# Layer norm's mean moved from the activations into the output weights, z's lower halves on VectorE, and a new order of the first phase

## The chip, the cores and the metric

One Trainium2 chip, one of its cores. The metric is the device time of one launch in microseconds (us); three runs of the kernel before gave 1175.65, 1175.5 and 1172.25 us, median 1175.5 us. Engines: PE (TensorE, matrix products), DVE (VectorE), ACT (ScalarE), POOL (GpSimd), and SP (SyncE), which issues the DMAs.

## The reference, cut to what matters

```python
def _moe_ref(x, w_in, w_out, g_ln):          # x: 4608 x 512, the attention's output
    h = x @ w_in                             # 4608 x 1024
    e = np.exp(h - np.max(h, axis=-1, keepdims=True))
    sm = e / (np.sum(e, axis=-1, keepdims=True) + 1e-09)
    solu = h * sm
    mu = np.mean(solu, axis=-1, keepdims=True)
    var = np.mean((solu - mu) ** 2, axis=-1, keepdims=True)
    ln = (solu - mu) / np.sqrt(var + 1e-06) * g_ln
    return ln @ w_out                        # 4608 x 512

def _moe2_ref(x, w_in, w_out):
    h = x @ w_in                             # 4608 x 2048
    return (h / (1 + np.exp(-1.702 * h))) @ w_out
```

Ahead of `_moe_ref` stands attention of 8 batches x 8 heads over keys and values pooled by 8; `_moe2_ref` takes its output. Inputs come in float64 for the weights, which the kernel takes as pairs of 32-bit words.

## The kernel before, in words

**Two phases.** The first does the attention, the first layer (`_moe_ref`) and the preparation of the second layer's weights; its 4608 tokens go in 36 tiles of 128, and two tiles make a `Pair`. The second phase is the second layer, in 6 blocks of 768 tokens, as products of 2x2 blocks by a seven-product scheme; its instructions have lines of their own (L1385 for its matrix products), and its program is written out by hand.

**Products in halves.** A float32 operand is split into a float16 upper half (`hi`) and a float16 lower half (`lo`, what the upper one leaves), and a product is three float16 products (`PASSES`). A product of float32 operands, used for scores and for sums over the pooled keys, appears as two records in the trace.

**One tile of the first phase.** Scores on PE into bank `psx`; softmax on DVE, ACT and POOL; the split attention goes through a transposing DMA (`aT`); PE makes the attention's output in `psv`; ACT and DVE split it into `xT`. `Pair.hidden` multiplies `xT` by `w1i` into one of two banks `psh` (24 products), DVE takes the row maximum `hmx` and its scaled negative `nm`, ACT the exponential `he`, DVE the product `tt` and its sum `mean`, ACT the sum of squares `vs`. `Pair.norm` makes the factor `a` on POOL, column by column of two; then, for each tile, ACT writes `tt = a * tt + mean` (mean is by then multiplied by -a), ACT copies the upper half into `zs[:, 0]`, and the lower half is a subtraction on POOL or DVE, whichever the planner finds free first. A transposing DMA turns both tiles' `zs` into `zT`, and `Pair.project` multiplies it by the output weights `w1o` (four groups of 24 products in a pair) into bank `psy`, near the end of the phase every second half into `psv`. There is one `psy`; the pooled sums of keys and values of batches 1 and 2 use it too, as do some of the products with `ones` that spread a maximum over the partitions.

**The output weights.** `second_weight` loads `w_out` in four parts, joins the words of each (`joined`, ending on POOL), finds the largest value, and `first_half` writes `w1o` for eight blocks of 128 rows: upper half on ACT, scaled by `gs` (g times the power of two), lower half on DVE.

**The order.** The first phase is put in order when the program is built. Each piece of work is a `Strand` of operations; `Plan.run` repeatedly takes the operation with the lowest score, made of the start that the planner's costs give, of the strand's due time, and of a random draw. `DRAWS` lists stretches of planned time with the size and the seed of the draw. So any edit to an operation, a cost or a seed changes the order on all engines. Each engine and SP's queue then work strictly in that order. On one line each, all operations of this phase are emitted by `op` (L496), `D` (L528) and `T` (L537), so that the profile tells them apart by their tiles only.

Of the kernel before, what the change touches and what calls it, by code (L numbers as in the profile page):

```python
# [84 lines left out]
DRAWS = ((70e3, 600, 13), (200e3, 150, 4), (330e3, 150, 13), (1e9, 150, 1))  # L85
# [4 lines left out]
LN_UP = 2.0 ** 10  # L90
# [93 lines left out]
class Plan:  # L184
# [13 lines left out]
    def start(self, steps, due):  # L198
        s = Strand(self, steps, due)
        self.strands.append(s)  # L200
        return s
# [95 lines left out]
def moe_kernel(ctx: ExitStack, tc: tile.TileContext, qT, kT, vT, w_in, w_out, g_ln, w2_in, w2_out, eye, outT):  # L297
# [138 lines left out]
    with ExitStack() as ph:  # L436
# [22 lines left out]
        def until(*strands):  # L459
            return lambda: all(s.ended for s in strands)  # L460
# [257 lines left out]
        def second_weight(due):  # L718
            n = 4
            am, a1, alln, gs = s1("w1o_am", n), s1("w1o_a1"), s1("w1o_all"), s1("w1o_gs", K1)  # L720
            measured = [None] * n

            def scale():
                yield lambda: all(measured)
                yield V("tensor_reduce", out=a1, in_=am, axis=AX.X, op=ALU.max)
                yield from largest(a1, alln, WIDE_LEAST)
                yield from whole_scale(alln, w1o_up, w1o_dn)
                yield g_done.over
                yield V("tensor_scalar_mul", gs, g_col, w1o_up)

            def part(i):
                raw = yield raw_new(2, DM)
                yield raw_load(raw, w_out, i, DM, 2)
                join = start(joined(raw.rearrange("p q f t -> p (q f) t"), lambda: measured[i]), due + 4 * i)
                two = [
                    start(
                        first_half(
                            join, raw[:, j], scaled.over, gs[:, 2 * i + j : 2 * i + j + 1], 2 * i + j,
                            slice(0, WC), w1o,
                        ),  # L740
                        due + 4 * i,
                    )
                    for j in range(2)
                ]

                def measure():
                    yield absmax_op(am[:, i : i + 1], high_words(raw), axis=AX.XY)
                    measured[i] = True

                start(measure(), DUE_MAX_OUT)  # L750
                yield until(*two)
                drop(raw)

            scaled = start(scale(), due)
            yield until(*[start(part(i), due + 4 * i) for i in range(n)])

# [69 lines left out]
        def values(b, due):  # L826
# [3 lines left out]
            yield from largest(am, alln, TINY, b < 2)  # L830
# [123 lines left out]
        class Pair:  # L954
# [53 lines left out]
            def norm(self):  # L1008
# [10 lines left out]
                yield G("tensor_tensor", out=q, in0=q, in1=q, op=ALU.mult)  # L1019
                yield G("tensor_tensor", out=v, in0=q, in1=self.vs, op=ALU.add)  # L1020
                yield G("tensor_tensor", out=r, in0=v, in1=minus_half, op=ALU.pow)
# [4 lines left out]
                yield G("tensor_tensor", out=self.mean, in0=self.mean, in1=a, op=ALU.mult)  # L1026
# [3 lines left out]
                for j in range(2):  # L1030
                    s = slice(j, j + 1)
                    tt = self.tt[j]
                    yield A(out=tt, in_=tt, func=AF.Identity, scale=a[:, s], bias=self.mean[:, s])
                    zs = yield New(sb, [P, 2, DF1], F16, "zs", bufs=2)
                    yield A(out=zs[:, 0], in_=tt, func=AF.Copy)
                    yield VG("tensor_tensor", out=zs[:, 1], in0=tt, in1=zs[:, 0], op=ALU.subtract)
                    drop(tt)
                    both.append((zs, (self.zT[:, :, j * P : (j + 1) * P], zs.rearrange("p a c -> p (a c)"))))
# [686 lines left out]
```

## Time and profile before

| | |
|---|---|
| runs | 1175.65, 1175.5, 1172.25 us; median 1175.5 us |
| the profiled execution | 1171.0 us, of it 1169.0 us from the first to the last instruction (the span) |
| PE busy in the span | 1125.7 us (96%) |
| DVE, ACT, POOL busy | 724.4, 754.7, 617.7 us (62%, 65%, 53%) |
| first phase, last product of a `zT` | ends at 510.7 us |
| granted clock of PE, mean | 0.994 |

A tile is named by the program's name without its number. `x8` behind an instruction is a count. In a list over time the bracket at the end tells how long the engine had been idle before and what ended that; in a list of groups, the two numbers after the bar are the busy time in us and the mean of one in ns. Matrix products are pipelined, so that one in a run takes less than its own mean.

### The profile page before, as it was taken

What the parts mean: (1) busy time and instruction counts of PE and PEld (TensorE: products, weight loads), DVE (VectorE), ACT (ScalarE), POOL (GpSimd) and SP (SyncE); (2) the same over time, 40 slices, a digit from 0 to 9 for tenths busy, and PEclk for the clock granted to TensorE, in tenths of its full rate; (3) what the DMA queues carried; (4) which work ended last, traced back from release to release, by engine and by line L of the source; (5) the groups of instructions that cost most, each with busy time, mean ns of one, the idle gap of its engine ahead of it and who ended that gap; (6) DMA issues with size and microseconds to landing.
All of it is one profiled execution on the core that took longest, in us unless ns stands there. A gap on an engine that the chain in (4) does not pass through costs nothing.

```text
span 1169.0 us, 19696 instructions
## 1 busy us (share of the span) xinstructions
PE 1125.7 (96%) x7737; PEld 726.1 (62%) x7737; DVE 724.4 (62%) x1105; ACT 754.7 (65%) x997; POOL 617.7 (53%) x643
## 2 busy tenths in 40 slices
PE   4888999999999999999999999999999999999998
PEld 4555676667676667765566656666666665566655
DVE  7988888777677753426753773567266636753650
ACT  6889998989798874737624752674367337625740
POOL 4566999989999985315503530561056016403530
PEclk9989999999999999999999999999999999999999
DMA  9979999999999768355465355536453653463131
GB/s 356 277 191 278 243 280 282 278 275 273 270 244 226 178 172 262 85 195 193 146 200 174 125 176 163 180 127 202 142 174 126 214 178 127 149 202 117 60 121 60
DMA packets 247356, 225.75 MB, mean 193 GB/s; under 512 B 165728, under 2 KB 218080, under 8 KB 246752
## 3 DMA queue, kind: packets, MB, share of 16 engines
q1 hardware_dynamic: 247264, 224.50, 67.0%
q8 instruction: 60, 0.98, 0.3%
q14 instruction: 32, 0.26, 0.1%
HBM read 151.06 MB, written 33.55 MB: 158 GB/s over the span
## 4 chain that ended last, share of the span: by engine, by line
PE 69%; POOL 13%; ACT 6%; DVE 5%; DMA 5%; issue 2%; SPq 1%; POOLq 0%; ACTq 0%; DVEq 0%
PE bank_a L1385 31%; PE bank_d L1385 16%; PE bank_b L1385 8%; PE psy L537 6%; PE psh L537 5%; POOL w_f L496 3%; PE psv L537 2%; POOL lo L496 2%; POOL zs L496 2%; POOL st L496 1%; POOL e L496 1%; PE psx L537 1%; DMA w2i_dram<-lo 1%; POOL q L496 1%; DMA raw<-w_out 1%
## 5 line engine op out<-in xcount | busy, mean ns | idle before, releaser
L1385 PEld LDWEIGHTS <-w2o 128*128 128x128 f16 x2016 | 197.0, 98 | 130.4
L1385 PEld LDWEIGHTS <-w2i 128*128 128x128 f16 x1974 | 193.1, 98 | 129.9 <-issue 2.4
L349 POOL TENSOR_TENSOR w_g<-w_g 128x384 f32<-128x384 f32 x42 | 46.1, 1097 | 399.2 <-ACT w_g L1464 399.2
L1479 DVE SCALAR_TENSOR_TENSOR g<-w_g,gu_b,g 128x1152 f16<-128x1152 f32 (+1 forms) x96 | 175.4, 1828 | 92.0 <-ACT g L1474 91.7
L1385 PE MATMUL bank_a<-ys,w2i 128*128 128x384 f16 x1128 | 205.6, 326 | 0.9 <-ACT c L1404 0.9
L537 PE MATMUL psh<-w1i,xT 128*128 128x512 f16 x864 | 201.8, 384 | 3.5 <-ACT xT L496 3.1
L1385 PE MATMUL bank_a<-g,w2o 128*128 128x384 f16 x1152 | 201.6, 326 | 0.0
L537 PEld LDWEIGHTS <-w1o 128*128 128x128 f16 x1728 | 168.0, 98 | 30.8 <-DMA zT<-zs 2.8
L537 PE MATMUL psy<-zT,w1o 128*128 128x256 f16 x1536 | 176.2, 273 | 3.5 <-DMA zT<-zs 2.3
L1474 ACT ACTIVATE g<-w_g,gu_b 128x1152 f16<-128x1152 f32 (+1 forms) x96 | 134.3, 1411 | 50.3 <-POOL w_g L352 39.3
L1404 ACT ACTIVATE c<-bank_a 128x384 f32<-128x384 f32 x188 | 90.7, 483 | 102.4 <-PE bank_a L1385 101.8
L537 PEld LDWEIGHTS <-xT 128*128 128x128 f16 x864 | 83.4, 99 | 96.3 <-issue 6.0
L1385 PE MATMUL bank_d<-g,w2o 128*128 128x384 f16 x576 | 104.2, 326 | 0.0
L496 POOL TENSOR_TENSOR zs<-tt,zs 128x1024 f16<-128x1024 f32 x36 | 78.4, 2178 | 44.2 <-ACT zs L496 43.8
L1385 PE MATMUL bank_d<-ys,w2i 128*128 128x384 f16 x564 | 101.1, 326 | 0.0
L1464 ACT ACTIVATE w_g<-c,ch_b 128x1536 f32<-128x1536 f32 x47 | 73.8, 1570 | 28.7 <-DVE c L1407 28.7
L352 POOL TENSOR_TENSOR w_g<-w_g 128x384 f32<-128x384 f32 x42 | 83.2, 1982 | 0.0
L1407 DVE SCALAR_TENSOR_TENSOR c<-bank_d,c 128x384 f32<-128x384 f32 x94 | 51.9, 552 | 41.9 <-ACT c L1404 29.6
L496 POOL TENSOR_TENSOR lo<-w_f,hi 128x512 f16<-128x512 f32 (+1 forms) x48 | 65.8, 1389 | 6.6 <-ACT e L496 2.9
L496 DVE TENSOR_REDUCE hmx<-psh 128x1 f32<-128x1024 f32 x36 | 43.8, 1218 | 36.2 <-PE psh L537 36.2
L537 PE MATMUL psx<-kbd,qt 128*128 128x144 f32 (+1 forms) x320 | 47.8, 312 | 15.1 <-ACT kbd L496 9.6
L496 DVE CUSTOM_DVE_ANT_0 tt<-psh,he 128x1024 f32<-128x1024 f32 x36 | 43.8, 1218 | 23.1 <-ACT he L496 22.9
(205 smaller groups left out, 1606.8 us busy)
## 6 DMA issues: line engine op xcount, KB each, us to landing
w2i<-w2i_dram SPq DMA_DIRECT2D x48, 896.0 KB, 4.6
w2o<-w2o_dram SPq DMA_DIRECT2D x84, 512.0 KB, 3.7
half<-kT SPq DMA_DIRECT2D x16, 576.0 KB, 6.4
half<-vT SPq DMA_DIRECT2D x16, 576.0 KB, 6.2
qt<-qT SPq DMA_DIRECT2D x36, 256.0 KB, 4.7
y_dram<-y SPq DMA_DIRECT2D x36, 256.0 KB, 3.5
y<-y_dram SPq DMA_DIRECT2D x48, 192.0 KB, 4.0
raw<-w_in SPq DMA_DIRECT2D x16, 512.0 KB, 7.7
```

The lines of the kernel that those rows point to most:

```text
L349: eng.tensor_tensor(out=w[:, 1], in0=q[:, Q12], in1=q[:, Q11], op=ALU.subtract)
L352: eng.tensor_tensor(out=w[:, 3], in0=q[:, Q21], in1=w[:, 2], op=ALU.subtract)
L496: getattr(eng, name)(*args, **kw)
L537: nc.tensor.matmul(*p[:3], start=p[3], stop=p[4], skip_group_check=len(p) > 5)
L1385: nc.tensor.matmul(bank, self.weight(p, kk, w), self.data(p, kk, i), start=(first and kk == 0 and w == 0 and i == 0), stop=(last and kk == ...
L1404: nc.scalar.activation(out=self.c[:, i], in_=getattr(self, bank), func=AF.Copy, scale=self.scale)
L1407: nc.vector.scalar_tensor_tensor(out=self.c[:, i], in0=getattr(self, bank), scalar=self.scale, in1=self.c[:, i], op0=ALU.mult, op1=ALU.add,)
L1464: nc.scalar.activation(out=self.w[:, 0:4], in_=self.c, func=AF.Gelu_apprx_sigmoid, scale=self.ch)
L1474: nc.scalar.activation(out=self.g[s.start][:, 0], in_=self.w[:, s], func=AF.Copy, scale=self.gu)
L1479: nc.vector.scalar_tensor_tensor(out=self.g[s.start][:, 1], in0=self.w[:, s], scalar=self.gu, in1=self.g[s.start][:, 0], op0=ALU.mult, op1 ...
```

## The change

Three things are changed in the first phase; the second phase's text is the same.

1. `second_weight` no longer scales and splits each part by itself. After the parts are joined, ACT writes `g_rows` (minus g over 1024, each value broadcast over 128 columns), PE multiplies it with the joined weights in eight float32 products of 128 x 512 into `psy`, so that every row of `psy` holds minus the column mean of g times w_out. ACT scales that by `w1o_up`. For each of the eight blocks DVE then writes the weight times `gs` plus `psy`, ACT copies the upper half, and POOL or DVE subtracts for the lower half. `psy` is given back after the last block.
2. `Pair.norm` no longer subtracts the mean: the pass `tt = a * tt + mean` is gone, ACT's copy into `zs[:, 0]` has the scale `a`, and the lower half is a `scalar_tensor_tensor` on DVE alone (tt times a minus the upper half). On POOL the product of mean and a is gone; a square of the mean and two short steps that keep the variance above a floor come in ahead of the power.
3. `DRAWS` has other stretches and seeds, a spread maximum of the output weights and of the second batch's values uses `psv` instead of `psy`, and `LN_UP` is 1.

```diff
-DRAWS = ((70e3, 600, 13), (200e3, 150, 4), (330e3, 150, 13), (1e9, 150, 1))
+DRAWS = ((70e3, 600, 5), (400e3, 150, 5), (430e3, 150, 813651), (1e9, 150, 495492))
...
-LN_UP = 2.0 ** 10
+LN_UP = 1.0
+LEVEL = 2.0 ** -18
...
-                yield from largest(a1, alln, WIDE_LEAST)
+                yield from largest(a1, alln, WIDE_LEAST, False)
...
-            def part(i):
+            def load(i):
                 raw = yield raw_new(2, DM)
                 yield raw_load(raw, w_out, i, DM, 2)
-                join = start(joined(raw.rearrange("p q f t -> p (q f) t"), lambda: measured[i]), due + 4 * i)
-                two = [
-                    start(
-                        first_half(
-                            join, raw[:, j], scaled.over, gs[:, 2 * i + j : 2 * i + j + 1], 2 * i + j,
-                            slice(0, WC), w1o,
-                        ),
-                        due + 4 * i,
-                    )
-                    for j in range(2)
-                ]
+                joins.append(start(joined(raw.rearrange("p q f t -> p (q f) t"), lambda: measured[i]), due + 4 * i))
+                words[i] = raw
...
+            yield g_done.over
+            rows = yield New(kv, [P, K1, P], F32, "g_rows", bufs=1)
+            yield A(out=rows, in_=g_col.unsqueeze(2).to_broadcast([P, K1, P]), func=AF.Copy, scale=-1.0 / DF1)
+            yield lambda: len(joins) == n and joins[0].ended
+            ps = yield New(psy, [P, 2, YB], F32, "psy", "psy")
+            level = ps.rearrange("p a c -> p (a c)")
+            for i in range(n):
+                yield joins[i].over
+                yield T(
+                    [
+                        (level, rows[:, 2 * i + j], words[i][:, j, :, 0].bitcast(F32), i + j == 0, i + j == n)
+                        for j in range(2)
+                    ]
+                )
+            drop(rows)
+            yield scaled.over
+            yield A(out=level, in_=level, func=AF.Copy, scale=w1o_up)
+
+            def levelled(i, j):
+                k = 2 * i + j
+                word = words[i][:, j, :, 0].bitcast(F32)
+                yield V(
+                    "scalar_tensor_tensor", out=word, in0=word, scalar=gs[:, k : k + 1], in1=level, op0=ALU.mult,
+                    op1=ALU.add,
+                )
+                yield A(out=w1o[0][:, k], in_=word, func=AF.Copy)
+                yield VG("tensor_tensor", out=w1o[1][:, k], in0=word, in1=w1o[0][:, k], op=ALU.subtract)
...
-            yield from largest(am, alln, TINY, b < 2)
+            yield from largest(am, alln, TINY, b < 1)
...
+                yield G("tensor_tensor", out=r, in0=self.mean, in1=self.mean, op=ALU.mult)
                 yield G("tensor_tensor", out=v, in0=q, in1=self.vs, op=ALU.add)
+                for j in range(2):
+                    s = slice(j, j + 1)
+                    yield G(
+                        "tensor_scalar", out=v[:, s], in0=r[:, s], scalar1=LEVEL, scalar2=v[:, s], op0=ALU.mult, op1=ALU.max
+                    )
...
-                yield G("tensor_tensor", out=self.mean, in0=self.mean, in1=a, op=ALU.mult)
...
-                    yield A(out=tt, in_=tt, func=AF.Identity, scale=a[:, s], bias=self.mean[:, s])
                     zs = yield New(sb, [P, 2, DF1], F16, "zs", bufs=2)
-                    yield A(out=zs[:, 0], in_=tt, func=AF.Copy)
-                    yield VG("tensor_tensor", out=zs[:, 1], in0=tt, in1=zs[:, 0], op=ALU.subtract)
+                    yield A(out=zs[:, 0], in_=tt, func=AF.Copy, scale=a[:, s])
+                    yield V(
+                        "scalar_tensor_tensor", out=zs[:, 1], in0=tt, scalar=a[:, s], in1=zs[:, 0], op0=ALU.mult,
+                        op1=ALU.subtract,
+                    )
```

Where the order moves: DVE's queue of before, at the place where the output weights' lower halves are written. `raw` is a part of `w_out`, `w1o_130` the lower halves, `mx` and `e` belong to the scores of a tile, `ISA tt` is the product with the exponential.

```order
L496 TENSOR_SCALAR w1o_gs<-g_col,w1o_up 128x8
L496 ISA tt,mean<-psh,he 128x1024
L496 ISA mean 128x1
L496 SCALAR_TENSOR_TENSOR w1o_130<-raw,w1o_gs,w1o_129 128x512 x8
L496 TENSOR_TENSOR e<-psx,mx 128x576
L496 TENSOR_SCALAR mean<-mean 128x1
L496 TENSOR_REDUCE hmx<-psh 128x1
L496 TENSOR_SCALAR nm<-hmx,h_sc 128x1
```

DVE's queue now, at the same work: the eight blocks read `psy` and are spread among scores and lower halves `zs`.

```order
L497 SCALAR_TENSOR_TENSOR zs<-tt,a,zs 128x1024
L497 SCALAR_TENSOR_TENSOR xT<-psv,xT 128x512
L497 TENSOR_SCALAR nm<-hmx,h_sc 128x1
L497 RECIPROCAL rs<-rs 128x8
L497 ISA tt,mean<-psh,he 128x1024
L497 ISA mean 128x1
L497 TENSOR_SCALAR mean<-mean 128x1
L497 SCALAR_TENSOR_TENSOR xT<-psv,xT 128x512
L497 SCALAR_TENSOR_TENSOR raw<-raw,w1o_gs,psy 128x512 x2
L497 TENSOR_REDUCE mx<-psx 128x8
L497 TENSOR_TENSOR e<-psx,mx 128x576
L497 SCALAR_TENSOR_TENSOR raw<-raw,w1o_gs,psy 128x512 x2
```

The first of the eight now stands behind a scaling on ACT, and with it behind the eight products on PE; two of the `zs` have come ahead of it.

ACT's queue of before, at the end of the first phase: `y` copies a projection out of its bank, `ys` are the second phase's first tokens, `c_kept` results of its first products.

```order
L496 ACTIVATE ys<-w_y_5978,y_up 128x4x384
L496 ACTIVATE y<-psy 128x512
L496 ACTIVATE ys<-w_y_5979,y_up 128x4x384
L496 ACT_TABLE_LOAD
L496 ACTIVATE ready<-y_up 128x1
L496 ACTIVATE y<-psv 128x512
L496 ACTIVATE c_kept<-psx 128x384 x2
L496 ACTIVATE y<-psy 128x512
L496 ACTIVATE y<-psv 128x512
L496 ACTIVATE c_kept<-psx 128x384 x2
```

ACT's queue now, at the same place.

```order
L497 ACTIVATE ys<-w_y_6173,y_up 128x4x384
L497 ACTIVATE ys<-w_y_6174,y_up 128x4x384
L497 ACT_TABLE_LOAD
L497 ACTIVATE ready<-y_up 128x1
L497 ACTIVATE y<-psy 128x512
L497 ACTIVATE y<-psv 128x512
L497 ACTIVATE c_kept<-psx 128x384 x4
```

Two of the second phase's first results stood ahead of the last pair's projection; now all four stand behind it.

## Rows read from the trace of the kernel before

**Rows 1.** Stretches: length; busy PE, PEld, DVE, ACT, POOL; PE clock; DMA share; GB/s
```profile
0.00:102.00 102.00, 72.86 (x478) 50.58 (x478) 87.87 (x168) 82.57 (x120) 56.96 (x70) 0.95 0.96 276
102.00:500.00 398.00, 388.78 (x3150) 273.90 (x3151) 274.24 (x502) 328.08 (x474) 336.34 (x406) 1.00 0.96 238
570.00:1169.00 599.00, 595.57 (x3663) 357.89 (x3661) 328.13 (x401) 303.16 (x355) 192.03 (x143) 1.00 0.46 151
```
**Rows 2.** PE in order of time, 88 to 117 us: start, us, what
```profile
102.08 5.41 PE L537 MATMUL psy<-zT,w1o 128*128 128x256 f16 x48 [2.34 <-DMA zT<-zs]
107.43 0.64 PE L537 MATMUL psv<-aT,vst 128*64 128x128 f16 x16
107.99 1.25 PE L537 MATMUL psx<-kbd,qt 128*128 128x144 f32 x8
```
**Rows 3.** What PE waited for, 102 to 570 us: total us, times, longest
```profile
PE psv L537 <- DVE xT L496: 3.9, 5, 1.7
PE psv L537 <- DVE w2all L496: 2.2, 1, 2.2
PE psx L537 <- ACT c_kept L496: 0.6, 1, 0.6
```
**Rows 4.** PE in order of time, 54 to 61 us: float32 products of the pooled sums
```profile
55.74 4.08 PE L537 MATMUL psy<-half,eye_t 128*128 128x144 f32 x32
```
**Rows 5.** Groups by form, 0 to 560 us: count | busy us, mean ns | idle before
```profile
L496 ACT ACTIVATE tt<-tt,mean,a 128x1024 f32<-128x1024 f32 x36 | 44.5, 1237 | 1.9 <-POOL mean L496 1.8
L496 ACT ACTIVATE zs<-tt 128x1024 f16<-128x1024 f32 x36 | 38.0, 1054 | 0.6
L496 ACT ACTIVATE vp<-psy 128x288 f32<-128x288 f32 x2 | 0.8, 406 | 0.5 <-PE psy L537 0.5
L496 POOL TENSOR_TENSOR zs<-tt,zs 128x1024 f16<-128x1024 f32 x36 | 78.4, 2178 | 44.2 <-ACT zs L496 43.8
L496 POOL TENSOR_TENSOR lo<-w_f,hi 128x512 f16<-128x512 f32 x32 | 37.9, 1192 | 6.5 <-ACT e L496 2.9 <-ACT rs L496 2.4 <-DMA w2i_dram<-lo 1.2
L496 POOL TENSOR_SCALAR q<-hsm 128x2 f32<-128x2 f32 x18 | 5.4, 301 | 1.5
L496 DVE SCALAR_TENSOR_TENSOR raw<-raw 128x1024 int32<-128x1024 int32 x22 | 34.0, 1546 | 3.3 <-ACT raw L496 3.3
L496 DVE TENSOR_REDUCE w2am<-raw 128x1 f32<-128x1024 f32 x16 | 19.3, 1209 | 3.8 <-DMA raw<-w_out 3.8
L496 DVE SCALAR_TENSOR_TENSOR xT<-psv,xT 128x512 f16<-128x512 f32 x36 | 24.7, 687 | 12.4 <-ACT xT L496 12.1
L496 DVE SCALAR_TENSOR_TENSOR w1o<-raw,w1o_gs,w1o 128x512 f16<-128x512 f32 x8 | 5.4, 744 | 0.0
L496 DVE TENSOR_TENSOR e<-psx,mx 128x576 f32<-128x576 f32 x35 | 26.4, 755 | 3.5 <-POOL st L496 2.2
L496 DVE TENSOR_REDUCE vam<-vp 128x1 f32<-128x288 f32 x8 | 3.5, 434 | 0.0
L496 DVE TENSOR_SCALAR pw_v<-v_all 128x1 int32<-128x1 int32 x8 | 1.2, 151 | 0.1
```
**Rows 6.** ACT in order of time, 74 to 83 us
```profile
73.40 1.20 ACT L496 ACTIVATE he<-psh,nm,h_sc 128x1024 f32<-128x1024 f32 x1
77.12 5.38 ACT L496 ACTIVATE w1o<-raw,w1o_gs 128x512 f16<-128x512 f32 x8 [2.42 <-DVE w1o_gs L496]
```
**Rows 7.** DVE and POOL in order of time, 399 to 402 us
```profile
399.75 2.22 DVE L496 SCALAR_TENSOR_TENSOR raw<-raw 128x1024 int32<-128x1024 int32 x1
...
399.74 1.15 POOL L496 TENSOR_TENSOR e<-e,rs 128x576 f32<-128x576 f32 x1 [0.24 <-ACT raw L496]
400.84 1.18 POOL L496 TENSOR_TENSOR q<-q 128x2 f32<-128x2 f32 x1
```
**Rows 8.** Stretches, columns as in Rows 1
```profile
29.00:117.00 88.00, 74.77 (x549) 49.67 (x549) 79.11 (x166) 78.26 (x117) 53.29 (x69) 0.94 0.99 249
146.00:292.00 146.00, 142.47 (x1148) 100.33 (x1146) 114.36 (x204) 129.29 (x189) 136.66 (x161) 1.00 1.10 278
```

More of the change, by code (lines that the diff above doesn't have):

```diff
@@ L720, in second_weight @@
             am, a1, alln, gs = s1("w1o_am", n), s1("w1o_a1"), s1("w1o_all"), s1("w1o_gs", K1)
-            measured = [None] * n
+            measured, words = [None] * n, [None] * n
             def scale():
@@ L750, in part @@
                 start(measure(), DUE_MAX_OUT)
+            joins = []
+            scaled = start(scale(), due)
+            for i in range(n):
+                start(load(i), due + 4 * i)
+            yield g_done.over
[4 more added lines that the diff above has]
+            level = ps.rearrange("p a c -> p (a c)")
+            for i in range(n):
+                yield joins[i].over
[17 more added lines that the diff above has]
+                yield VG("tensor_tensor", out=w1o[1][:, k], in0=word, in1=w1o[0][:, k], op=ALU.subtract)
+            for i in range(n):
+                two = [start(levelled(i, j), due + 4 * i) for j in range(2)]
                 yield until(*two)
-                drop(raw)
-            scaled = start(scale(), due)
-            yield until(*[start(part(i), due + 4 * i) for i in range(n)])
+                drop(words[i])
+            drop(ps)
         BY_PRODUCT = (1, 2)
```

## The prediction

> **What bounds the kernel now.** I read the busy time by stretches first, then PE over time around the first projection, then what PE waited for. The stretches [rows 1] show two regimes. From 102 us on PE is hardly ever idle: 388.8 of 398 us up to 500, and 595.6 of 599 in the second phase, whose text the change leaves alone. Up to 102 us it is idle for 29.1 of 102 us, and there DVE (87.9) and ACT (82.6) are the busy ones. The hinge is the first projection, at 102.08 us [rows 2]; from there on PE has enough work in stock. So the time is PE's work, plus what PE idles until its stock is filled, plus 9.2 us of small waits later, half of which DVE ends: 3.9 us in five waits for `xT`, 2.2 us in one for a maximum of the second weights [rows 3]. The large sums that the change takes off ACT and POOL are not on this path after 102 us; they count only where they bring the first projection forward or end one of the small waits.
>
> **What is removed, off the path.** ACT loses 36 passes of 1.24 us, 44.5 us; its copy gets a scale, and so takes between the copy's 1.05 and the old pass's 1.24 us, at most 6.6 us in all. POOL loses 36 subtractions of 2.18 us, 78.4 us [rows 5]. In the norm one short POOL step goes and three come, 0.6 us a pair at 0.30 each [rows 5]; the chain from the sums to `zs` loses far more than that. I take nothing for all this directly: PE hides it, being busy. If that cover went, a `zs` chain would be shorter by about 2 us (1.24 and the 0.63 to 0.97 between POOL's 2.18 and the price on DVE, below, less 0.6).
>
> **The lower halves on DVE.** No row has this operation with both operands of these types. The nearest is the join of raw words, also 128 x 1024 with two operands in SBUF: 1.55 us on the mean [rows 5]. Below, a pass over 1024 columns is 1.21 us (`w2am`); above, one join took 2.22 us beside a busy POOL [rows 7]. I take 1.55: 36 make 56 us more on DVE, of which four fall ahead of the first projection.
>
> What the 2.22 us is, [rows 7] show: the join starts at 399.75, 0.01 us behind a POOL product of 1.15 us, and the POOL step behind that, otherwise 0.2 to 0.3 us, takes 1.18 and ends as the join does. The two take turns. The Trainium skill (SBUF — State Buffer, Who interferes with whom) states this as a rule: a VectorE instruction with two SBUF inputs contends with a GpSimd one that reads SBUF, and the one that issues second waits in full. The trace agrees here; the mean of 22 joins is well under a full wait each, so I hold to 1.55, and the rule taken to its end is the third rival.
>
> **The column means.** Eight float32 products of 512 columns are 16 records. Thirty-two records of 144 columns took 4.08 us [rows 4], 0.1275 each; by columns 0.453, so 7.25 us of PE. They stand, with ACT's scaling, ahead of the first projection, where PE idles 29.1 us: cost of the products themselves nothing, 7.25 us if that cover is gone. What they do cost is a wait on DVE: the first of the eight levelled blocks stands behind ACT's scaling and so behind all products, and behind it in DVE's queue stand two tiles' scores and the subtractions for `zs`, for which PE waits. Bounds: 0, if what stands ahead in the queue covers it, and 7.9 (all products and a scaling of about 0.6, as a copy of 512 columns out of PSUM, which DVE does in 0.69 [rows 5]). In before, the nearest wait is ACT's for the factors `gs` at this very place, 2.42 us [rows 6]; I take 2.4. The blocks themselves, 0.744 each before [rows 5], I leave as they are; their subtractions go to POOL, 8 x 1.19 = 9.5 us, and run beside DVE on an engine with 45 us idle up to 102 [rows 1].
>
> **When the first projection comes.** In the new order `psy` holds the column means until the last block, then the pooled keys' or values' sums; ACT's copy `vp` frees it, and that copy stands behind the exponential of the fifth tile, which needs DVE's `nm`. I count DVE's queue up to that `nm` against its queue up to 102 us of before. More: four `zs`, 6.2 us, and two `xT`, 1.4. Less: four `w2am` and a product `tt` at 1.21, 6.05; an `e`, 0.76; a `vam`, 0.43; six short steps at 0.15, 0.9 [rows 5]. Net -0.5. With DVE's idle time unchanged (14.1 us of the 102), the wait of 2.4, then ACT's exponential of 1.20 with 0.2 for its sum [rows 6] and the copy of 0.41 [rows 5]: 102.1 - 0.5 + 2.4 + 1.8 = 105.8, **3.7 us later**. But by then PE has, in the new order, done the same six hidden tiles, two tiles more in `psv` (0.64 each) and one more in `psx` (1.25) [rows 2]: 2.5 us less to do behind it.
>
> **The rest of the first phase.** Of the 9.2 us idle between 102 and 500 I take a third away, 3 us: ACT and POOL, 89% and 94% busy from 146 to 292 us [rows 8], lose a good part, while waits for DVE stay. Bounds: 9.2 us gained, and about 10 lost (third rival). At the end of the phase two of the four first results of the second phase move behind the last projection; each product into `psx` there waits for ACT to copy the one before, 0.6 us [rows 3], now twice in a row instead of once: +0.6. The last pair's `zT` then has eight groups of projections as cover, as before, without the 3.9 us or so of second-phase products; its chain has become shorter, as said, and I take nothing.
>
> **Sum.** +3.7 - 2.5 - 3 + 0.6 = **-1.2 us**. The profiled execution took 1171.0 us (span 1169.0 and 2.0 around it), 0.4% under the median of 1175.5; the difference is put on the median: 1174.3 us. A measurement of this kernel can tell about 0.3%, 3.5 us, from no change, so this is no change.
>
> **The rivals.**
> - *Faster: the start is packed better.* DVE and ACT have 14.1 and 19.4 us idle in the first 102 [rows 1], and the passes that go were links in the chain. If the new order halves DVE's 14.1, the hinge comes 7 us earlier, and with ACT and POOL relieved 5 instead of 3 us of the later waits go: -1.2 - 7 - 2 = -10.2, **1165 us**. For it: no engine but DVE is fuller. Against it: DVE's work ahead of the hinge is the same, and from 29 to 117 us it is 90% busy already [rows 8].
> - *Slower: PE has to wait for the column means' products.* If PE reaches the hinge as late as if they were uncovered, 7.25 instead of 2.4 and the copies of pooled sums behind them late too: about +6, **1180 us**. For it: one `psy`, held through the products and all eight blocks. Against it: 29.1 us of idle time at that place.
> - *Slower: DVE and POOL block each other.* From 146 to 292 us DVE is 114.4 us busy [rows 8]. About 13 of the 36 `zs` fall there (36 x 146 / 398). At 1.55 us they bring it to 134.5, 92%; at 2.2, as in [rows 7], to 143, 98%. From 29 to 117 us DVE was 90% busy and PE idle for 13.2 of 88 us, 15% [rows 8]. If PE's idle share in the middle, now 2.4%, goes half-way to that, it loses 7.5 us more there and gains no 3; the four early `zs` cost 2.6 more: -1.2 + 3 + 7.5 + 2.6 = +11.9, **1187 us**. It decides from a mean `zs` of about 1.9 us on. For it: POOL still has its products of two SBUF operands, and the same wait hits POOL. Against it: POOL loses 78 us of just such work, so a collision becomes less likely.
>
> The Trainium skill's rule above (SBUF — State Buffer, Who interferes with whom), taken in full for each `zs`, gives this last rival; the 22 joins bear it out only now and then.
>
> **How the numbers follow.** Forecast (within 0.3%, 1172 to 1179): 0.42. Packed better: 0.33. Products uncovered: 0.10. Blocking: 0.15. Faster by over 0.3% 0.33, within 0.3% 0.42, slower 0.25. The forecast's own range is 1171 to 1178, from 0 to 7.9 of the DVE wait and some us of small waits. As cases of both signs hold more than half, the range runs from the faster rival's 1164 to just under the blocking one's, 1185.
>
> **What would show it.** Groups by form: a mean `zs` on DVE of 1.3 to 1.7 us; at 1.9 or more the third rival holds. PE over time: first projection between 103 and 109 us with the column means' products ahead of it, over 7 to 8 us of PE; at 99 or less the first rival holds. PE idle from 102 to 500 us of 5 to 8 us; more than 12, ended by DVE, would make the forecast wrong. At the end two short waits of `psx` for `c_kept`. The second phase, from 570 us to the end, unchanged at 599 us within 1 us; if it moves, I have missed a cause.

## The result and the profile after

The changed kernel takes 1182.7 us (median of 6 runs, 1180.4 to 1185.3) against 1173.4 us for the kernel before (6 runs beside it, 1172.3 to 1175.7): a ratio of 1.0081, 95% interval 1.0063 to 1.0098. It is slower by 9.3 us, inside the range given (1164 to 1185), but on the side that had a chance of 0.25: 1174.3 had been forecast (1.2 below the 1175.5 of the first three runs of before), with no change as the likeliest case. The profiled execution took 1182.8 us with a span of 1180.7, so the spans differ by 11.7 us.

The stretches of the changed kernel, columns as in [rows 1]:

```profile
0.00:102.00 102.00, 74.09 (x466) 47.95 (x467) 80.32 (x150) 77.34 (x117) 61.44 (x75) 0.95 0.85 251
102.00:500.00 398.00, 383.41 (x3089) 268.59 (x3088) 312.13 (x532) 290.23 (x446) 297.21 (x415) 1.00 0.96 240
570.00:1180.70 610.70, 607.28 (x3737) 365.07 (x3734) 334.62 (x408) 312.07 (x364) 199.50 (x149) 1.00 0.45 151
```

In the middle row, from 102 to 500 us, ACT and POOL lost 38 and 39 us, as they should, and DVE gained 38. PE's idle time went from 9.2 to 14.6 us [rows 1]. Three moments of PE after the change, in order of time: the second tile's scores, the column means' products and the first projection.

```profile
18.89 2.26 PE L538 MATMUL psx<-kbd,qt 128*128 128x144 f32 x8 [5.08 <-issue]
...
82.77 7.43 PE L538 MATMUL psy<-raw,g_rows 128*128 128x512 f32 x16
...
110.49 1.69 PE L538 MATMUL psy<-zT,w1o 128*128 128x256 f16 x14 [0.17 <-ACT vp L497]
```

The first projection starts at 110.49 us instead of 102.08 [rows 2]. PE's work of the second phase, before and after (the range after the durations is the first and last start; first row before, second row after):

```profile
L1385 PE MATMUL bank_a<-ys,w2i x1128: 322/326/326, 514.2 to 1116.9; 128*128 128x384 f16 x188
```

```profile
L1418 PE MATMUL bank_a<-ys,w2i x1128: 322/326/326, 526.3 to 1128.6; 128*128 128x384 f16 x188
```

The first product into `bank_a` starts 12.1 us later, and from there to the end of the span both take the same (654.8 and 654.4 us). So the whole loss lies ahead of it: 8.4 us up to the first projection, and 3.7 behind it, although some 2.5 us of work had been pulled ahead of it. Between the two moments PE idles 9.7 us before and 15.7 us after (length less busy PE; columns as in [rows 1], first row before, second row after):

```profile
102.08:514.20 412.12, 402.40 (x3265) 285.04 (x3265) 274.71 (x503) 330.67 (x478) 336.26 (x406) 1.00 0.93 232
```

```profile
110.49:526.30 415.81, 400.07 (x3225) 282.08 (x3225) 314.96 (x537) 295.93 (x450) 290.26 (x409) 1.00 0.93 233
```

What PE waits for after the change (totals, times, longest, 102 to 570 us, to be held against [rows 3]):

```profile
PE psv L538 <- DVE xT L497: 4.1, 5, 1.7
PE psv L538 <- DVE w2all L497: 2.5, 2, 1.6
PE psy L538 <- ACT y L497: 2.2, 2, 1.4
PE psv L538 <- DMA raw<-w_out: 2.1, 1, 2.1
PE psv L538 <- DMA aT<-st: 1.3, 1, 1.3
PE psx L538 <- ACT c_kept L497: 1.2, 2, 0.6
PE psv L538 <- DVE v_all L497: 1.1, 1, 1.1
PE psv L538 <- DVE mean L497: 1.0, 1, 1.0
```

And the waits of before, between 102 and 500 us, that [rows 3] leave out, but for the one that ends at the first projection:

```profile
PE psy L537 <- ACT y L496: 1.1, 2, 0.7
PE psv L537 <- DVE v_all L496: 1.0, 2, 0.7
PE psx L537 <- DMA qt<-qT: 0.7, 1, 0.7
```

DVE ends 8.7 us of PE's waits after the change, in short waits spread over nine places. But it ended 7.1 us of them before (3.9, 2.2 and 1.0). Of the 5.4 us that PE idles more from 102 to 500 us, the waits that DVE ends grew by 1.6 only; those that ACT ends grew by 1.3 (1.1 to 2.4, with 0.2 at the first projection), those that a DMA ends by 2.7 (0.7 to 3.4). The engine that a wait names last is not yet the one that made it long; the runs below bear on that. The groups that answer to [rows 5]:

```profile
L497 DVE SCALAR_TENSOR_TENSOR zs<-tt,a,zs 128x1024 f16<-128x1024 f32 x36 | 59.2, 1660 | 14.1 <-ACT zs L497 11.7 <-POOL q L497 1.5 <-POOL h_sc L497 0.8
L497 DVE TENSOR_REDUCE w2am<-raw 128x1 f32<-128x1024 f32 x16 | 19.3, 1212 | 5.7 <-DMA raw<-w_in 3.0 <-DMA raw<-w_out 2.7
```

The lower halves cost 1.66 us each on DVE. DVE also stands 5.7 us in front of the second weights' measurements, waiting for their loads; before, 3.8 [rows 5].

### The profile page after: what moved, and what is told of

It reads as the page before. It is cut to its first block, busy times and chain, and to the rows that moved or that the text cites. A ratio compares the mean times of both kernels' runs of the same rounds, so it can differ in the third digit from the quotient of the medians.

```text
span 1180.7 us, 19741 instructions
## 1 busy us (share of the span) xinstructions
PE 1132.6 (96%) x7753; PEld 727.0 (62%) x7753; DVE 765.5 (65%) x1133; ACT 721.1 (61%) x977; POOL 583.1 (49%) x657
## 4 chain that ended last, share of the span: by engine, by line
PE 71%; POOL 9%; DVE 8%; ACT 4%; DMA 4%; issue 3%; SPq 1%; POOLq 0%; DVEq 0%; ACTq 0%
PE bank_a L1418 31%; PE bank_d L1418 15%; PE bank_b L1418 8%; PE psh L538 7%; PE psy L538 6%; PE psv L538 3%; POOL w_f L497 2%; PE psx L538 2%; POOL e L497 1%; DVE zs L497 1%; POOL lo L497 1%; DVE raw L497 1%; POOL st L497 1%; DMA w2i_dram<-lo 1%; DMA qt<-qT 1%
## 5 line engine op out<-in xcount | busy, mean ns | idle before, releaser
L497 POOL TENSOR_TENSOR lo<-w_f,hi 128x512 f16<-128x512 f32 (+1 forms) x48 | 69.3, 1468 | 16.5 <-DMA w2i_dram<-lo 7.7
L497 DVE SCALAR_TENSOR_TENSOR zs<-tt,a,zs 128x1024 f16<-128x1024 f32 x36 | 59.2, 1660 | 14.1 <-ACT zs L497 11.7
L497 POOL TENSOR_TENSOR st<-e,st 128x576 f16<-128x576 f32 x35 | 48.9, 1399 | 20.4 <-ACT st L497 20.2
```

The lines of the kernel that those rows point to most:

```text
L497: getattr(eng, name)(*args, **kw)
```

## The experiments

Eighteen kernels were run. The kernel before took 1171.4 to 1173.5 us beside them, depending on the chip, so ratios are compared; 0.1% is 1.2 us. Where a kernel is said to keep an order, the sequence in which the planner of before, or of the changed kernel, emitted its operations is written into it as a list, and each engine's queue is that of the original row for row, but for the edit. The code below is cut to what an edit changes; in `b_norm`, `b_nott` and `a_zsG` constants that keep the values in range (`LN_UP`, the scale of the product `tt`) change along with it. The theories: **Z**, the lower halves on DVE make its queue late; **C**, the second weight's new making costs; **O**, the order drawn anew is at fault.

### The norm's edits in the old order

Three kernels: only the lower halves on DVE (`b_zs`), those and no pass `tt` (`b_norm`), only no pass `tt` (`b_nott`).

```
-  VG("tensor_tensor", out=zs[:, 1], in0=tt, in1=zs[:, 0], op=subtract)           # b_zs, b_norm
+  V("scalar_tensor_tensor", out=zs[:, 1], in0=tt, scalar=..., in1=zs[:, 0], mult, subtract)
-  A(out=tt, in_=tt, func=Identity, scale=a, bias=mean)                           # b_norm, b_nott
```

> The kernel before with every instruction of every engine in its place as before; only z's 36 lower halves move from POOL (2178 ns each) to DVE, as the scalar_tensor_tensor that the changed kernel uses (here with the factor 1.0, since the values are already normalised). Theory O (the newly drawn order costs the 9 us): before's time, 1173.4 +- 2 us, as DVE has room. Theory Z (the lower halves on DVE make DVE's queue late for PE): 1177 to 1183 us, with PE's idle time from 102 to 500 us up from 9 to 13 us or more. Theory C (the eight column-mean products are 7.4 us of uncovered PE work): before's time, since they are not in it.

> The kernel before in its own order with both edits of the norm: ACT's pass tt<-tt is left out and z's lower half is made by DVE with the factor. The mean over the columns is not subtracted anywhere, so that part of the computation is left out. 36 ACT passes of 1.24 us (44 us of ACT) and 36 POOL passes (78 us) go, 36 DVE passes come (about 60 us). Theory O: 1171 to 1174 us. Theory Z: 1176 to 1182 us, less what the missing ACT passes give back, 1 to 3 us. Theory C: 1171 to 1174 us.

> The kernel before in its own order with ACT's pass tt<-tt left out (36 of 1.24 us) and z's lower half still on POOL; the mean is not subtracted and the lower half has no factor, so z is not whole. If the 4.9 us between the two earlier runs in this order (with the pass 1183.6, without it 1178.7) are worth the same when DVE is free of the lower halves: 1167 to 1169 us. If ACT's passes were only late because DVE was (theory Z alone): 1171 to 1173.5 us.

Measured: `b_zs` 1.0096 (1.0080 to 1.0112), `b_norm` 1.0054 (1.0041 to 1.0067), `b_nott` 0.9986 (0.9973 to 0.9998). Of 11 us for the lower halves on DVE, the missing ACT pass gives 5 back; with the lower halves on POOL the same missing pass gives 1.6, hardly clear of nothing (0.2 to 3.2). All three times lie where theory Z had them, `b_zs` at the top of its range or just above it. PE's waits in `b_zs`, 102 to 570 us, and the group:

```profile
PE psv L674 <- DVE xT L633: 10.1, 8, 2.0
PE psy L674 <- ACT y L633: 4.9, 5, 2.5
PE psh L674 <- DVE mean L633: 2.3, 1, 2.3
```

```profile
L633 DVE SCALAR_TENSOR_TENSOR zs<-tt,zs 128x1024 f16<-128x1024 f32 x36 | 51.4, 1429 | 11.0 <-ACT zs L633 10.4 <-DMA vst<-vx 0.3
```

The same instructions in the same places, and the waits for `xT` are 10.1 us against 3.9 [rows 3]. One of the eight places, DVE first and then PE:

```profile
366.17 1.52 DVE L633 SCALAR_TENSOR_TENSOR zs<-tt,zs 128x1024 f16<-128x1024 f32 x1
...
368.81 0.68 DVE L633 SCALAR_TENSOR_TENSOR xT<-psv,xT 128x512 f16<-128x512 f32 x1
```

```profile
369.54 0.23 PE L674 MATMUL psv<-diag,ones 128*128 128x128 bf16 x1 [1.92 <-DVE xT L633]
```

A lower half that PE does not wait for stands in DVE's queue ahead of an `xT` for which PE waits 1.92 us; the kernel before has 0.51 us there. At other of these places no `zs` stands directly in front, and the queue is late from further back. Theory Z holds in this order, at a mean of only 1.43 us for each `zs`. That ACT's gain counts mainly where DVE has made ACT late (5 against 1.6 us) fits these three runs, and is not shown further.

### The second weight in the old order

`b_level` has the part on `second_weight` of the diff and nothing else; `b_all` has all edits of the computation. Operations that the old list lacks are put in as soon as they can start, and an old one that misses its buffer is put off. `b_work` makes the second weight as before and does the new operations on a tile of its own:

```
+  for i in range(4): T([(level, rows[:, 2*i + j], word, ...) for j in range(2)])
+  A(out=level, in_=level, scale=w1o_up)
+  for k in range(8): V("scalar_tensor_tensor", out=more, in0=word, scalar=gs[k], in1=level, mult, add)
+                     A(out=two[:, 0], in_=more);  VG("tensor_tensor", out=two[:, 1], ..., subtract)
```

> The kernel before with the second weight made as in the changed kernel (eight column-mean products on PE, the added row scaled by ACT, DVE's multiply-add, ACT's copy, POOL's or DVE's lower half); the norm stays as before, and every other instruction keeps the old order, put off only where a buffer is not yet free. Theory C (the second weight's new making costs): the first projection goes from 102 to 106 us or later and the raw buffers come free later, 1177 to 1183 us. Theories Z and O: the old order has room for it, 1172 to 1176 us.

> All edits of the computation of the changed kernel, in the old order with the new instructions put in where they can start. Theory O (the newly drawn order is the worse one): 1175 to 1180 us. Theories Z and C (the edits cost whatever the order): the sum of the parts in the old order, the norm's +6.5 us and the second weight's, so 1179 to 1188 us, no better than the 1182.7 us of the changed kernel.

> The kernel before in its own order, with the second weight made as before (raw buffers given back as before), and the new instructions of the column means done beside it on a tile of their own, for nothing that is used: eight 128x512 products, ACT's scaling, eight DVE multiply-adds, eight ACT copies, eight POOL or DVE subtractions, and the psy bank held while they last. Theory H (what cost 24.5 us when the second weight was made the new way in this order is that its four raw buffers are held some 24 us longer, so that the next weight's loads and DVE's measuring of them come late): 1174 to 1180 us, with the loads at 80 us as before and no wait over 4 us on xT at 130 us. Theory W (the added instructions themselves cost): 1190 to 1198 us.

Measured: `b_level` 1.0206 (1.0182 to 1.0230), `b_all` 1.0326 (1.0308 to 1.0344), `b_work` 1.0136 (1.0119 to 1.0153). All three missed every range given: `b_level` came at 1198.0 us, 15 above theory C's 1183, and `b_all` at 1211.5, 23 above the 1188 given for Z and C. DVE in `b_level` at the two places that matter, and what comes of it on PE:

```profile
99.65 1.41 DVE L634 SCALAR_TENSOR_TENSOR raw<-raw,w1o_gs,psy 128x512 f32<-128x512 f32 x2 [6.92 <-ACT psy L634]
...
118.35 1.22 DVE L634 TENSOR_REDUCE w2am<-raw 128x1 f32<-128x1024 f32 x1 [10.49 <-DMA raw<-w_in]
```

```profile
133.26 1.06 PE L675 MATMUL psv<-aT,vst 128*64 128x128 f16 x16 [16.34 <-DVE xT L634]
```

DVE stands 6.9 us before the first levelled block, since the products and ACT's scaling are not done, and 10.5 us before a measurement whose load is late: the four `raw` buffers are held until the blocks are written. The loads of `w_in` for the second layer, first in the kernel before, then in `b_level` (SP's queue):

```profile
80.23 5.26 SPq L528 DMA_DIRECT2D raw<-w_in  x6
```

```profile
104.22 9.69 SPq L666 DMA_DIRECT2D raw<-w_in  x8
```

Behind both stands the `xT` for which PE waits 16 us. `b_work` gives the buffers back as before (its loads go out at 80.81 us), and still loses 16 of the 24 us:

```profile
101.51 0.75 DVE L634 SCALAR_TENSOR_TENSOR more<-beside,w1o_gs,psy 128x512 f32<-128x512 f32 x1 [6.05 <-ACT psy L634]
```

Neither theory had its time, 1188.0 us. DVE's queue waits for the chain of products, scaling and multiply-add here too, with the buffers given back, and in `b_work` the bank `psy` is held longer too (first projection at 127.94 us), so the 16 and 8 us are no clean split. What is shown is that the old order, with the chain put in as early as it can start, is a bad one for it: all edits cost 38 us in it, and the newly drawn order brings that down to 9.3. Other places for the chain in the old order were not tried.

### The changed kernel in its own order

`a_level1` leaves out seven of the eight column-mean products, `a_raw5` has a fifth `raw` buffer, `a_start` takes SP's first nine loads in the order of the kernel before, `a_zsG` puts the lower halves back on POOL.

```
-  yield T([(level, rows[:, 2*i + j], words[i]..., i+j == 0, i+j == n) for j in range(2)])   # a_level1
+  if i == 0: yield T([(level, rows[:, 0], words[0]..., True, True)])
-  RAWS = 4                                                                                  # a_raw5
+  RAWS = 5
-  kT kT qt eye vT raw_z qt raw_z vT                                                         # a_start
+  kT kT vT eye qt raw_z raw_z vT qt
-  V("scalar_tensor_tensor", out=zs[:, 1], in0=tt, scalar=a, in1=zs[:, 0], mult, subtract)   # a_zsG
+  G("tensor_tensor", out=zs[:, 1], in0=tt, in1=zs[:, 0], op=subtract)
```

> The changed kernel in its own order, with seven of the eight column-mean products left out (the first alone stands, so the column means are not whole). Theory C: 7/8 of 7.43 us go from the end, 1176 +- 1.5 us, with the first projection at 104 us instead of 110.5. Theories O and Z: the products lie under other waits, 1181 to 1183 us, and PE waits instead where they stood.

> The changed kernel in its own order with five raw buffers instead of four. Theory H in the new order too: the first load of the second layer's weight goes out at 80 to 90 us instead of 97, DVE's measuring (w2am) waits less for raw, 1177 to 1181 us. Rival (in the new order the loads are no longer what PE waits for): 1181.5 to 1184 us.

> The changed kernel in its own order, but SP's first nine loads in the order of the kernel before (kT, kT, vT, eye, qt, raw_z, raw_z, vT, qt). If the order of the first loads is what makes PE start 2 to 3 us later, and if that delay reaches the end: first psx at 9.6 us, first projection at 107.5, 1179 to 1180.5 us. If DVE's and ACT's queues swallow it before the first projection: 1182 to 1184 us.

> The changed kernel in its own order, with z's 36 lower halves moved back from DVE (59.2 us) to POOL's subtraction as before (about 78 us); the factor is left out of the lower half, and the values are scaled down by a power of two, so z's lower halves are not whole. Theory Z (the lower halves on DVE cost in the new order as in the old one): 1173 to 1177 us, and PE's waits ended by DVE after the first projection fall from 9 us to 4 or less. Theory O (in the new order the waits come from loads that DVE stands behind and from other DVE work): 1180 to 1184 us. A third: POOL, which the new order did not plan for, becomes late: above 1184 us, with waits ended by POOL.

Measured: `a_level1` 1.0106 (1.0090 to 1.0122), `a_raw5` 1.0078 (1.0063 to 1.0093), `a_start` 1.0082 (1.0067 to 1.0097), `a_zsG` 1.0155 (1.0127 to 1.0184), to be held against the changed kernel's 1.0081.

Without 6.3 us of products the kernel is not faster but, if anything, slower (1184.5 us; theories O and Z had 1181 to 1183), and its first projection comes at 111.08 us. PE reaches the next product of scores earlier and waits there for DVE (first rows `a_level1`, second rows the changed kernel):

```profile
94.50 2.26 PE L676 MATMUL psx<-kbd,qt 128*128 128x144 f32 x8 [4.95 <-DVE e L635]
96.55 5.50 PE L676 MATMUL psh<-w1i,xT 128*128 128x512 f16 x18
```

```profile
96.28 1.22 PE L538 MATMUL psx<-kbd,qt 128*128 128x144 f32 x8 [0.45 <-DVE e L497]
97.34 4.05 PE L538 MATMUL psh<-w1i,xT 128*128 128x512 f16 x18
```

PE's clock at that place, stretches of `a_level1`, columns as in [rows 1]:

```profile
90.00:94.50 4.50, 0.00 (x0) 0.03 (x1) 3.69 (x6) 2.77 (x7) 3.98 (x10) 0.79 0.90 224
94.50:97.00 2.50, 2.50 (x10) 2.13 (x11) 1.92 (x4) 2.50 (x4) 2.21 (x4) 0.50 0.07 17
```

After 4.5 idle us the granted clock is 0.50, 1.2 instead of 2.4 GHz. The scores take 2.26 us instead of 1.22, and the 18 hidden products behind them 5.50 instead of 4.05. The longer wait (4.5 us) and the slower clock (2.5 us) together take back the 6.3 us. Without the slower clock some 1.8 us would be left at this place, an estimate from these rows. So theory C, as far as the products go, is at most a small part in this order; the rest of the chain, scaling and multiply-adds, was not taken out of it.

The fifth buffer and the first loads change nothing that can be measured in the time. (Their first projections come at 108.71 and 108.62 us all the same: 2 us at this moment in one profile each say nothing on the time.) With the fifth buffer the first load goes out at 92.69 us instead of 97.09, not at 80. With the old first loads the first scores come at 10.0 instead of 11.54 us, but the second only at 18.51, and the start stays 3 us late. That delay is the draw's: the old text under the new draws (`b_drawsA`, below) has its second scores at 18.81 too, and the changed text under the old draws (`a_drawsB`) has them at 15.56, before 15.85.

`a_zsG` has the time of the third case of its expectation, with POOL busy 337.9 of 398 us and DVE 263.8. But none of PE's waits from 102 to 500 us has POOL for its last releaser; DVE and ACT end them, so that POOL makes them late is likely and not shown. Moving the work back into an order that was not drawn for it says little on DVE. So the lower halves were made cheap in place instead, alone and together with `a_level1`'s edit:

```
-  V("scalar_tensor_tensor", out=zs[:, 1], in0=tt, scalar=a, in1=zs[:, 0], mult, subtract)   # a_zscopy
+  V("tensor_copy", zs[:, 1], zs[:, 0])
```

> The changed kernel in its own order, with z's 36 lower halves made by a DVE copy of the upper half (half-precision to half-precision) instead of the multiply-subtract on 32-bit values, so z's lower halves hold the wrong values; every instruction keeps its place in its queue. 59.2 us of DVE become some 15 to 25. Theory Z in the new order: the DVE-ended waits of PE after the first projection fall from 9 to 4 us or less, 1174 to 1178 us. Theory P (a new order takes its waits from where it was drawn, and no one instruction holds them): 1179 to 1183 us.

> Both at once: z's lower halves by a cheap DVE copy and only one of the eight column-mean products (z's lower halves and the column means are not whole). If the two parts hide each other (each alone gives nothing since the other still bounds the start): 1170 to 1175 us, the first projection at 104 us. Theory P: 1178 to 1184 us.

Measured: `a_zscopy` 1.0046 (1.0030 to 1.0062), `a_zscopy_level1` 1.0079 (1.0058 to 1.0100).

```profile
L635 DVE COPY zs<-zs 128x1024 f16<-128x1024 f16 x36 | 26.3, 735 | 19.4 <-ACT zs L635 19.3
```

33 us less of DVE give 4 us back. The idle time of PE from 102 to 500 us falls by 4.6 us to 10.0; the first projection (108.19) is no earlier than in the two kernels above whose time did not change. What PE waits for in `a_zscopy` between 102 and 500 us:

```profile
PE psv L676 <- DVE xT L635: 6.1, 3, 3.7
PE psv L676 <- DVE v_all L635: 2.6, 1, 2.6
PE psy L676 <- ACT y L635: 1.2, 1, 1.2
```

The time is the one given for theory Z (1174 to 1178; 1176.8 measured), its other sign is not: DVE still ends 8.7 us of waits, where 4 or less were expected. What went are waits that ACT and DMAs had ended. And POOL, beside a cheaper DVE, is busy 277.3 us from 102 to 500 instead of 297.2, so its relief may be in the 4 us as well. Theory Z has at most that share in the new order: some 4 of 9.3 us. Taking the products out as well loses those 4 us again, with the same wait (4.80 us on `e` at 93.59) as in `a_level1`. The two do not hide each other.

### What a draw is worth

The draws alone were exchanged between the two texts, and then both texts were drawn with two seeds that were chosen for neither.

```
-  DRAWS = (... 13), (... 4), (... 13), (... 1)         # b_drawsA: the changed kernel's; a_drawsB: the reverse
+  DRAWS = ((70e3, 600, s), (1e9, 150, s))              # b_seed21, a_seed21: s = 21; b_seed22, a_seed22: s = 22
```

> The text of the kernel before with the changed kernel's DRAWS, no other edit: the order is drawn anew with the same work. Theory O: a new draw costs by itself, 1177 to 1185 us, with the first projection at 104 us or later and PE's idle time after it above 12 us. Theories Z and C: 1171 to 1177 us.

> The text of the changed kernel with the old DRAWS. The old text under the new draws lost 25 us. If a draw is good only for the text that it was chosen for: 1192 to 1212 us. If the old draws also suit the new text, 1180 to 1186 us. If below 1175 us, the new draws are what made the change slower.

> The text of the kernel before, its order drawn with seed 21 (sizes 600 up to 70 us, 150 after), a draw that was chosen for neither text. With the same seed for the changed text it shows what the edits cost in orders that were not chosen: between 1185 and 1205 us; the difference changed less before +5 to +15 us if the edits themselves cost, -3 to +3 if only the choice of the draw did.

> The text of the changed kernel, its order drawn with seed 21 as the run beside it: 1190 to 1212 us; +5 to +15 us over that run if the edits themselves cost, -3 to +3 if only the choice of the draw did.

> The text of the kernel before under a second draw chosen for neither text (seed 22). With seed 21 the two texts came out at 1195.4 and 1196.6 us. If a draw's own luck is some 5 us to either side: 1188 to 1202 us.

> The changed text under seed 22. If the edits cost nothing that outweighs a draw's luck: within 6 us of the run beside it on either side, 1188 to 1203 us. If seed 21 hid a cost of the edits of 10 us: 10 us or more above the run beside it.

| draw | kernel before's text | changed text |
|---|---|---|
| its own | 1 | 1.0081 (1.0063 to 1.0098) |
| the other's | 1.0216 (1.0196 to 1.0235) | 1.0291 (1.0274 to 1.0308) |
| seed 21 | 1.0208 (1.0184 to 1.0233) | 1.0216 (1.0195 to 1.0238) |
| seed 22 | 1.0100 (1.0080 to 1.0120) | 1.0266 (1.0236 to 1.0296) |

Each text is best by 1 to 2% under its own draw, and a draw of one text is no good for the other. Under the three draws that are not their own, the texts average 1.0175 and 1.0258, 0.8% apart, as they are under their own; but the two pairs with one seed differ by 0.1% and 1.7%. That the edits cost whatever the order is likely by this, and not settled. Theory O's signs are all there in `b_drawsA` (first projection at 107.77, 20.4 us of idle PE from 102 to 500), but at 1198 us it lies above every range given, and it prices the new draws for the old text only: under them the changed text is the faster one.

## Why the prediction was wrong

**The step that failed** is the one on the rest of the first phase. It took 3 of 9.2 us of small waits away, since ACT and POOL lose so much, and put no price on DVE's 56 us more unless a `zs` took 1.9 us or longer. In the sum it stands at -3, with +0.6 for the end of the phase; behind the first projection PE idled 6.0 us more instead. Measured, PE's idle time between 102 and 500 us grew by 5.4 to 14.6 us, past the 12 that the prediction had named as making the forecast wrong. Both halves of the step are answered by runs: ACT's relief is worth 1.6 us with DVE free (`b_nott`), and DVE's load costs 11 us in the old order (`b_zs`, at a mean of 1.43) and at most some 4 in the new one (`a_zscopy`). DVE need not be full for that, nor collide with POOL each time: in `b_zs` it is busy 303.9 of 398 us, 76%, and half of its `zs` take 1.23 us or less. The prediction counted half of the 9.2 us as DVE's; it was 7.1 of them, so that DVE was the engine to ask about from the start.

**The first projection.** The second term that failed: forecast 105.8, it came at 110.49, outside the 103 to 109 given. The sum kept DVE's idle time at 14.1 us, plus one wait of 2.4. The stretch of the changed kernel up to the `nm` of that sum, that `nm`, ACT's exponential behind it, and the four kinds of wait for other engines that held DVE longest in the stretch:

```profile
0.00:108.03 108.03, 80.12 (x516) 52.30 (x517) 86.23 (x159) 81.60 (x123) 67.10 (x79) 0.95 0.86 254
```

```profile
107.83 0.20 DVE L497 TENSOR_SCALAR nm<-hmx,h_sc 128x1 f32<-128x1 f32 x1
```

```profile
108.76 1.19 ACT L497 ACTIVATE he<-psh,nm,h_sc 128x1024 f32<-128x1024 f32 x1
```

```profile
DVE hmx L497 <- PE psh L538: 3.6, 3, 1.5
DVE xT L497 <- ACT xT L497: 3.5, 3, 2.0
DVE mx L497 <- PE psx L538: 2.8, 3, 1.8
DVE rs L497 <- ACT rs L497: 1.6, 1, 1.6
```

DVE's `nm` ends at 108.03 instead of 104.0. DVE worked 86.2 us until then, 1.2 less than the sum has, and idled 21.8 us instead of 16.5; behind `nm` another 0.7 go, since ACT is at other work for as long. So the term that failed is DVE's idle time: it grew by 7.7 us in many short waits for PE and ACT, of which before had 2.3 us for `mx`, 0.7 for `xT`, 0.2 for ACT's `rs` and none for `hmx`. The wait of 2.4 at the first levelled block was none: the block starts at 93.10, as the `xT` ahead of it ends, for which DVE had waited 1.97 us.

Why the new order has these waits is open. PE starts 3 us late under the new draws (second scores at 18.89 instead of 15.85, first product into `psh` at 39.13 instead of 36.06, in `b_drawsA` at 39.50), and the order of the first loads alone is not the reason (`a_start`). But that this lateness reaches the first projection is not shown: DVE has worked as much by 40 us as before (30.6 and 30.2 us), and `a_raw5`, with its first `psh` later still (40.49), has its first projection 1.8 us earlier than the changed kernel. In these three kernels, whose times agree (the changed one, `a_raw5`, `a_start`), it lies between 108.6 and 110.5, so some 2 of the missing 4.7 us may belong to the one execution that was profiled.

**Two slips in the working,** without weight in the sum. The shorter `zs` chain comes to 1.3 to 1.6 us by the terms given, not about 2. And half-way from 2.4% to 15% of 146 us is 9.2 us more, not 7.5, so that the blocking rival would stand near 1189.

**What held.** The products take 7.43 us of PE (7.25 said), and leaving seven of them out gains nothing (`a_level1`): the rival of uncovered products falls, though its time, 1180 us, came near by luck. The work pulled ahead is near the 2.5 us said: PE's busy time ahead of the first projection grew by 9.55 us, 7.43 of it products, which leaves 2.1. A `zs` takes 1.66 us (1.55 taken, 1.3 to 1.7 given). The two waits for `c_kept` are there, 1.2 us in all, and the second phase is unchanged.

**The rivals.** The blocking one named the engine and the sign, but not the main lever. A `zs` meets POOL in just the way described, DVE and POOL of the changed kernel in order of time:

```profile
375.15 2.82 DVE L497 SCALAR_TENSOR_TENSOR zs<-tt,a,zs 128x1024 f16<-128x1024 f32 x1
...
374.73 2.15 POOL L497 TENSOR_TENSOR w_f<-sgw,raw 128x1024 f32<-128x1024 f16 x1
376.84 2.27 POOL L497 TENSOR_TENSOR st<-e,st 128x576 f16<-128x576 f32 x1
```

The `zs` is issued 0.42 us behind a POOL product and takes 2.82 us where the shortest takes 1.27; the POOL step behind it takes 2.27. The Trainium skill's rule (SBUF — State Buffer, Who interferes with whom), that the later of the two waits for the earlier, agrees with these rows. But at a mean of 1.66 us that is a part of the price, below the 1.9 from which this rival was to decide. The rival of a better packed start is refuted outright.

**What stays open.** The sum by steps is +8.4 up to the first projection, -2.3 for work already done, +6.0 of idle time, together the 12.1 us by which the second phase starts later in the profiled executions. The cheap copies give back 4 of the 9.3 us between the medians, DVE's and POOL's relief together. For the other 5 no single holder was found: not the buffers or the first loads, and the products at most in small part. The short POOL steps of the norm, the maxima moved to `psv`, and the scaling and multiply-adds in the new order were not run by themselves. The change needs another order, and how good the drawn one is can't be told apart from what the edits cost by themselves with three other draws of each text. No kernel that does the whole computation came out better than the kernel before.

## What to carry to other kernels

Work taken off an engine that PE hardly waits for and put on the one whose results it does wait for can be a loss, even if that engine is only 70% busy: 11 us in `b_zs`, in an order otherwise kept. Price it by what stands behind it in the queue, not by its busy share. When an edit comes with a newly drawn order, keep the emitted sequence as a list and try the edit in the old one: for an edit that only moves or drops work (`b_zs`, `b_norm`, `b_nott`) it separates the edit from the order. An edit that adds a chain of its own breaks the old order (38 us in `b_all`) and can't be priced that way. Where a forecast keeps an engine's idle time as it was although the order is new, that is the term to bound: here it grew from 14.1 to 21.8 us. And ask of a wait what made its last releaser late, not only which engine it names: the cheap copies on DVE took away waits that ACT and DMAs had ended.

## What the hardware showed beside this

Leaving out PE work can cost time: in `a_level1` the 4.5 us that PE then idled brought the granted clock to 0.50 for the 2.5 us behind it, scores that take 1.22 us took 2.26, and hidden products that take 4.05 took 5.50. On DVE, the multiply-subtract of 128 x 1024 32-bit values ran in 1.23 us on the median in `b_zs` (shortest 1.21, longest 2.60) and in 1.54 in the changed kernel (1.27 to 2.82), where its factor is a column and not a constant, and POOL is busy 297 of 398 us instead of 272. One price from one kernel does not carry over. A half-precision copy of the same shape took from 0.40 to 1.86 us, 0.74 on the mean, in the same 36 places.
